# Moving a DFT table set-up, load order and casts in a fused attention and long-convolution kernel

## The chip, the cores and the metric

The kernel runs on one core of a Trainium2 chip. The metric is the device time of one execution in microseconds (us), lower is better. The inputs lie in DRAM as float32; the output goes back as float32.

## The reference

Windowed attention with a few global keys, then a gated long convolution (a circular one, through an FFT over the 768 positions), for 4 batches:

```python
scores = scale * q @ k.T ; keep = is_global | is_local      # 8 global keys, 96 local ones
a = softmax(where(keep, scores + bias_by_head_and_distance, -1e9))
x = a @ v                       # (4, 768, 8 * 64)
proj = x @ w_proj               # 512 -> 3 * 512 : x1, x2, x3
X2 = rfft(x2, axis=1); H = rfft(filter_fft, axis=0)
y = x1 * irfft(X2 * H) * x3
return y @ w_out
```

## The kernel before, in words

**Attention.** A batch has 8 heads of 768 positions, taken as 4 pairs of heads. Keys are cut into 7 tiles of 128 rows: 8 global keys and 120 local ones each (EW, K0 give their widths and starts). The 8 rows of the global keys and values are the same in all tiles; only tile 0 gets them from DRAM, and one DMA on SP's queue copies them to tiles 1 to 6 (L110, `kt<-kt` and `vt<-vt`). A pair goes through transposes of q and k (L434, L459; in batch 0 L449), scores in three groups (L471) with one exp each on ACT (L478), a multiplication by a mask on DVE (L487, L490), two calls of `values` (L498, L503: the product with v and the row sums; then a reciprocal and a multiplication on DVE, L507, L508), and a transpose to `xT` (L515, copied by ACT at L516). After two pairs, DVE forms the sums and differences of the two halves of the sequence, `xa` and `xb` (L424, L425).

**Convolution ("hyena").** Six projections of `xa`, `xb` (L532) give x2; the DFT is a product with a table `fwd` (`forward`, L316, six slots, copied by ACT to `X` at L571); `product` and `sums` on DVE multiply by the filter's spectrum `h1`, `h2` (L558 to L568); the inverse is a product with the table `inv` (L602). Eight `gate` calls give x1 * x3: 8 matmuls each (L545), a scaling on ACT (L549) and a multiplication on DVE (L550). Then `w_out` (L620), a scaling on ACT (L623) and the stores on SP (L624). All six-way users of PSUM share three banks, the tag "mm".

**Tables.** `dft_angles`, `dft_fold` and `dft_sines` make `fwd`: outer products on TensorE (L235 to L241), a rounding copy on ACT (L245), two folding steps on DVE (L250, L253), a sine on ACT (L261, from another activation table than exp). `filter_stage` makes the spectrum (`filter_spectrum`: six `forward` calls on the filter's halves `f2`, each read by ACT and then by DVE) and the inverse tables (`inverse_tables`: transposes of `fwd`).

**Order.** It is written out by hand: each engine runs its instructions in the order in which the program emits them. `weave` merges streams: each has a number of chunks and a stretch from a to b on a common scale, and the chunk that is due first comes next. `after(n, fn)` puts DVE work off by n chunks. `emit` runs the tables first, then batch 0's attention (with `busy`, matmuls on zeros, in between), then for each b the convolution of batch b woven with the attention of batch b+1 (called stage b below). `load_batch(b+1)` is called right before stage b. Loads that change float32 to float16 are issued by GpSimd (POOL); batch 0's q and k come through SP's queue as float32 (`load_first`), six staging tiles for eight loads, and are cast by DVE and ACT (`cast_first`, L140).

A queue or an engine's instruction stream that waits holds all that is behind it. Line numbers are those of the kernel before, unless "now" stands with them.

## Time and profile before

| | |
|---|---|
| time, median of 2 runs | 254.11 us (253.55 to 254.67) |
| profiled execution | 254.49 us, of which its span 252.7 us |
| busy: TensorE (PE), VectorE (DVE) | 201.4 us (80%), 157.5 us (62%) |
| busy: ScalarE (ACT), GpSimd (POOL) | 143.2 us (57%), 78.4 us (31%) |
| DMA | 21.73 MB, mean 86 GB/s |
| mean granted TensorE clock | 0.946 of full speed |
| one load issued by GpSimd (L105) | 0.94 to 0.97 us |
| GpSimd's issues of batch 0's values, of a third of w_proj and of the filter | 6.0 to 15.3 us |

All times in the rows are us from the span's start. The page's shares are means over unlike parts: 11 us of set-up, 39 us of batch 0's attention, stages 0 to 2, and a last convolution that has no attention beside it. PE's busy time includes matmuls that run at half clock and the filling `busy` matmuls. A row of a timeline gives start, duration, engine, line, operation and operands, and in brackets how long the engine had stood idle and what ended it.

### The profile page before, as it was taken

What the parts mean: (1) busy time and instruction counts of PE and PEld (TensorE: products, weight loads), DVE (VectorE), ACT (ScalarE), POOL (GpSimd) and SP (SyncE); (2) the same over time, 40 slices, a digit from 0 to 9 for tenths busy, and PEclk for the clock granted to TensorE, in tenths of its full rate; (3) what the DMA queues carried; (4) which work ended last, traced back from release to release, by engine and by line L of the source; (5) the groups of instructions that cost most, each with busy time, mean ns of one, the idle gap of its engine ahead of it and who ended that gap; (6) DMA issues with size and microseconds to landing.
All of it is one profiled execution on the core that took longest, in us unless ns stands there. A gap on an engine that the chain in (4) does not pass through costs nothing.

```text
span 252.7 us, 4276 instructions
## 1 busy us (share of the span) xinstructions
PE 201.4 (80%) x1670; PEld 107.7 (43%) x1670; DVE 157.5 (62%) x333; ACT 143.2 (57%) x233; POOL 78.4 (31%) x100
## 2 busy tenths in 40 slices
PE   7871777778689779660998989959988989996884
PEld 2330544433345445330355645424644554453431
DVE  6774468725688988520269979714799793067340
ACT  5874247458355667440476577437665666663433
POOL 6960799996780000395820000000000000000000
PEclk9979579999999999995699999999999999999799
DMA  6999999999998000299990000250000004200006
GB/s 212 256 194 205 161 60 135 138 148 164 130 126 38 0 0 3 83 196 190 123 91 3 0 3 0 83 185 0 3 0 3 1 0 178 75 0 0 3 11 238
DMA packets 79628, 21.73 MB, mean 86 GB/s; under 512 B 71336, under 2 KB 76536, under 8 KB 79608
## 3 DMA queue, kind: packets, MB, share of 16 engines
q0 software_dynamic: 73584, 11.67, 70.9%
q1 hardware_dynamic: 6024, 9.79, 11.6%
q8 instruction: 13, 0.21, 0.4%
q14 instruction: 7, 0.06, 0.1%
HBM read 26.48 MB, written 6.29 MB: 130 GB/s over the span
## 4 chain that ended last, share of the span: by engine, by line
PE 31%; DVE 26%; POOL 15%; DMA 15%; ACT 6%; issue 5%; SPq 0%; POOLq 0%; DVEq 0%; ACTq 0%
PE pt L620 7%; PE pt L532 6%; DVE g L550 5%; PE pt L545 5%; POOL vt L105 5%; DMA fl<-in_moe_filter_fft_dram 5%; DMA kt<-kt 4%; DMA qt<-in_q_dram 3%; PE pt L316 3%; POOL kt L105 3%; DVE xn L508 3%; PE tx L515 2%; DMA kt<-in_k_dram 2%; POOL qt L117 2%; PE pt L602 2%
## 5 line engine op out<-in xcount | busy, mean ns | idle before, releaser
L545 PE MATMUL pt<-xT,w 128*128 128x384 f16 x256 | 47.9, 332 | 0.5 <-ACT dst L534 0.4
L545 PEld LDWEIGHTS <-w 128*128 128x128 f16 x256 | 23.8, 99 | 17.6 <-issue 4.2
L478 ACT ACTIVATE E_99<-sp 128x864 f16<-128x864 f32 x24 | 21.5, 898 | 12.4 <-PE sp L471 11.9
L478 ACT ACTIVATE E_96<-sp 128x864 f16<-128x864 f32 x24 | 21.4, 894 | 8.6 <-PE sp L471 6.2
L105 POOL DMA_DIRECT2D vt<-in_v_dram x28 | 26.0, 965 | 0.9 <-issue 0.6
L534 ACT CAST dst<-pt 128x512 f16<-128x512 f32 x24 | 14.0, 585 | 21.0 <-PE pt L532 20.8
L620 PE MATMUL pt<-wo,y 128*128 128x512 f16 x96 | 23.2, 380 | 2.8 <-DVE y L613 2.2
L571 ACT CAST X<-pt 128x512 f16<-128x512 f32 x24 | 14.1, 586 | 16.1 <-PE pt L316 15.9
L602 PE MATMUL pt<-inv,X 128*128 128x384 f16 x96 | 19.5, 334 | 3.8 <-DVE X L568 3.0
L623 ACT ACTIVATE t<-pt 128x512 f32<-128x512 f32 x24 | 14.3, 597 | 14.3 <-PE pt L620 14.1
L269 PE MATMUL pt<-idle 128*128 128x512 f16 x44 | 20.0, 511 | 1.2 <-DVE idle L645 1.2
L471 PE MATMUL sp<-QT,KT 64*128 64x216 f16 (+2 forms) x224 | 18.2, 254 | 3.5 <-ACT E_96 L478 1.8
L508 DVE TENSOR_TENSOR xn<-o,rc 128x448 f16<-128x448 f32 x32 | 20.0, 624 | 1.1
L105 POOL DMA_DIRECT2D kt<-in_k_dram x21 | 19.2, 938 | 4.6 <-DMA qt<-in_q_dram 3.4
L316 PE MATMUL pt<-dst,fwd 128*128 128x512 f16 x72 | 19.0, 380 | 0.0
L515 PE MATMUL tx<-ident,xn 128*128 128x128 f16 x112 | 8.9, 219 | 11.6 <-DVE QT L439 5.7
L516 ACT COPY xT<-tx 128x768 f16<-128x768 f16 x16 | 12.8, 799 | 9.4 <-PE tx L515 9.1
L460 DVE COPY KT<-tk 128x896 f16<-128x896 f16 x12 | 7.4, 619 | 14.4 <-PE tk L459 14.4
L459 PE MATMUL tk<-ident,kt 128*128 128x128 f16 x84 | 7.3, 225 | 11.3 <-DMA kt<-kt 11.3
L117 POOL DMA_DIRECT2D qt<-in_q_dram x18 | 16.0, 962 | 0.0
L471 PEld LDWEIGHTS <-KT 64*128 64x128 f16 x224 | 7.5, 95 | 19.2 <-issue 15.4
L604 ACT CAST eo<-pt 128x384 f16<-128x384 f32 x16 | 7.7, 484 | 12.7 <-PE pt L602 6.8
(228 smaller groups left out, 392.2 us busy)
## 6 DMA issues: line engine op xcount, KB each, us to landing
out_dram<-t SPq DMA_DIRECT2D x24, 256.0 KB, 2.1
vt<-in_v_dram POOLq DMA_DIRECT2D x24, 128.0 KB, 6.4
qt<-in_q_dram POOLq DMA_DIRECT2D x18, 128.0 KB, 6.7
kt<-in_k_dram POOLq DMA_DIRECT2D x18, 128.0 KB, 5.5
t<-in_q_dram SPq DMA_DIRECT2D x4, 384.0 KB, 6.7
t<-in_k_dram SPq DMA_DIRECT2D x4, 384.0 KB, 6.6
w<-in_moe_w_proj_dram POOLq DMA_DIRECT2D x3, 512.0 KB, 13.8
fl<-in_moe_filter_fft_dram POOLq DMA_DIRECT2D x1, 768.0 KB, 12.3
```

What stands on the lines that cost most here:

```text
L105: g.dma_start(dst[P - (hi - lo):P, t, :, 0:D], src[b, :, lo:hi, :].rearrange("h p d -> p h d"))
L117: g.dma_start(qt[:, t], self.q[b, :, P * t:P * t + P, :].rearrange("h p d -> p h d"))
L269: self.nc.tensor.matmul(pt, self.idle[:, 0:P], self.idle, start=True, stop=True)
L316: self.nc.tensor.matmul(pt, self.fwd[:, kt, s, :], src[:, kt, :], start=(kt == 0), stop=(kt == 2))
L471: nc.tensor.matmul(sp[:, hh, off:off + w], KT[64 * hh:64 * hh + 64, o:o + P], QT[64 * hh:64 * hh + 64, KL * m:KL * m + w], start=(off == 0 ...
L478: nc.scalar.activation(eo, sp[:, :, 0:432].rearrange("p h (m w) -> p h m w", m=2), Act.Exp, scale=self.scale)
L508: nc.vector.tensor_mul(xn[:, :, hh, :], o[:, :, 0:D], rc.to_broadcast([P, 7, D]))
L532: nc.tensor.matmul(pt, src[:, c, P * t:P * t + P], self.w[:, c, DM:2 * DM], start=(c == 0), stop=(c == 3))
L545: nc.tensor.matmul(pt[:, 0:h], self.w[:, c, o + P * j:o + P * j + P], xT[:, c, h * s:h * s + h], start=(c == 0), stop=(c == 3))
L602: nc.tensor.matmul(pt[:, 0:h], X[:, s, cs], self.inv[:, s, :], start=(s == slots[0]), stop=(s == slots[-1]))
L620: nc.tensor.matmul(pt, y[:, c, P * t:P * t + P], self.wo[:, c, :], start=(c == 0), stop=(c == 3))
L623: nc.scalar.mul(ot, pt, osc)
```

## The change

It does these things:

- `fwd` is made in `filter_stage`, within stage 0, its pieces woven between the first projections; the table of ACT loaded at the start is that of exp. `filter_stage` has 16 chunks from 0.0 to 0.4 (9 from 0.05 to 0.3 before), and the next attention starts at 0.4 of stage 0 (0.25 before). The filter's halves are formed by DVE, not POOL.
- In stage 0 all eight gates come right after the projections (`early`). Elsewhere the gate after the first pair of `forward` calls comes later, and `halves` is emitted ahead of its gate.
- The loads of batch b+2 are issued before stage b; those of batch 1, and two thirds of `w_proj`, right after batch 0's attention is emitted.
- Batch 0's value rows of the global keys are copied by DVE (one copy of 8 partitions by 3120 elements) in place of the DMA.
- The q and k casts of batch 0's pairs 2 and 3 are made by POOL.
- `values` calls come one or two chunks later than before; the attention in stages 1 and 2 is spread to 0.95 (0.9 before).
- Six `busy` matmuls at the start (2 and 10 before); `distances` first; `later` is kept sorted.

```diff
--- before.py
+++ after.py
@@ -107,8 +107,9 @@
             if t == 0:
                 g.dma_start(dst[0:NG, 0, :, 0:D],
                             src[b, :, 0:NG, :].rearrange("h p d -> p h d"))
-        self.nc.sync.dma_start(dst[0:NG, 1:7], dst[0:NG, 0:1].to_broadcast(
-            [NG, 6] + list(dst.shape[2:])))
+        if b > 0:
+            self.nc.sync.dma_start(dst[0:NG, 1:7], dst[0:NG, 0:1].to_broadcast(
+                [NG, 6] + list(dst.shape[2:])))
 
     def load_batch(self, b):
         g = self.nc.gpsimd
@@ -135,7 +136,9 @@
     def cast_first(self, hp):
         sq, sk = self.first[2 * hp:2 * hp + 2]
         out = []
-        for cp, src in ((self.nc.vector.tensor_copy, sq), (self.nc.scalar.copy, sk)):
+        pool = self.nc.gpsimd.tensor_copy
+        for cp, src in ((pool if hp > 1 else self.nc.vector.tensor_copy, sq),
+                        (pool if hp > 1 else self.nc.scalar.copy, sk)):
...
@@ -154,12 +157,14 @@
     def load_weights(self):
         g, cp, DM = self.nc.gpsimd, self.cp, self.DM
         self.w = cp.tile([P, 4, 3 * DM], F16)
-        wr = self.w_proj.rearrange("(t p) n -> p t n", p=P)
-        g.dma_start(self.w[:, :, DM:2 * DM], wr[:, :, DM:2 * DM])
+        self.wr = self.w_proj.rearrange("(t p) n -> p t n", p=P)
+        g.dma_start(self.w[:, :, DM:2 * DM], self.wr[:, :, DM:2 * DM])
         self.fl = self.mp.tile([P, 6, DM], F16, tag="g", bufs=2)
         g.dma_start(self.fl, self.filt.rearrange("(t p) n -> p t n", p=P))
-        g.dma_start(self.w[:, :, 0:DM], wr[:, :, 0:DM])
-        g.dma_start(self.w[:, :, 2 * DM:3 * DM], wr[:, :, 2 * DM:3 * DM])
+
+    def load_more_weights(self):
+        for o in (0, 2 * self.DM):
+            self.nc.gpsimd.dma_start(self.w[:, :, o:o + self.DM], self.wr[:, :, o:o + self.DM])
 
     def load_w_out(self):
         self.wo = self.cp.tile([P, 4, self.DM], F16)
@@ -240,8 +245,9 @@
                                  skip_group_check=True)
             nc.tensor.matmul(o, one, cst[:, None, 0:2, None].to_broadcast([1, 2, 2, r]),
                              start=False, stop=True, skip_group_check=True)
-        tag = ("y", "eo", "ab", "ab")[a]
-        th = self.mp.tile(list(an.shape), F32, tag=tag, bufs=2 if tag == "ab" else 1, name="th")
+        if a == 0:
+            self.th = self.mp.tile([P, 3, 512], F32, tag="y", bufs=1)
+        th = self.th[:, a] if a < 3 else self.mp.tile([P, 768], F32, tag="eo", bufs=1, name="th")
@@ -292,6 +298,7 @@
     def after(self, n, fn):
 
         self.later.append((self.chunk + n, fn))
+        self.later = deque(sorted(self.later, key=lambda x: x[0]))
...
-    def filter_halves(self):
-        f2 = self.mp.tile([P, 2, 3, self.DM], F16, tag="y", bufs=1)
-        self.nc.gpsimd.tensor_add(f2[:, 0], self.fl[:, 0:3], self.fl[:, 3:6])
-        self.nc.gpsimd.tensor_sub(f2[:, 1], self.fl[:, 0:3], self.fl[:, 3:6])
-        self.f2 = f2
-
     def filter_stage(self):
+        self.fwd = self.cp.tile([P, 3, 6, P], F16)
+        ths = []
+        for a in range(4):
+            ths.append(self.dft_angles(a))
+            for k in range(2):
+                self.after(k + 1, lambda k=k, a=a: self.dft_fold(k, *ths[a]))
+            yield 1
+        yield 1
+        yield 1
+        for a in range(4):
+            self.dft_sines(a, ths[a][0])
         yield from self.filter_spectrum()
         yield from self.inverse_tables()
 
@@ -332,6 +344,10 @@
 
 
         nc, cp, DM = self.nc, self.cp, self.DM
+        f2 = [self.mp.tile([P, 3, DM], F16, tag="stg", bufs=6, name="f2") for _ in range(2)]
+        nc.vector.tensor_add(f2[0], self.fl[:, 0:3], self.fl[:, 3:6])
+        nc.vector.tensor_sub(f2[1], self.fl[:, 0:3], self.fl[:, 3:6])
+        yield 1
         self.h1 = cp.tile([P, 6, DM], F16)
         self.h2 = cp.tile([P, 6, DM], F16)
         sc = 2.0 * H_SCALE
@@ -354,7 +370,7 @@
                 nc.vector.tensor_scalar(self.h2[0:64, s], pt[64:P], sc, None, op0=Alu.mult)
...
         for s in range(6):
-            self.forward(s, self.f2[:, 0], self.f2[:, 1], evac)
+            self.forward(s, f2[0], f2[1], evac)
             yield 1
 
 
@@ -404,13 +420,16 @@
         trk(0)
         yield 1
         for i in range(n + 1):
+            if first and i == 1:
+                self.nc.vector.tensor_copy(vt[0:NG, 1:7], vt[0:NG, 0:1].to_broadcast(
+                    [NG, 6, self.H, self.D + 1]))
             for live, fn in ((i < n, lambda: sc(i, 0)),
                              (i + 2 < n and first, lambda: cast(i + 2)),
-                             (i > 0, lambda: val(i - 1, 0)),
                              (i + 1 < n, lambda: trk(i + 1)),
                              (i < n, lambda: sc(i, 1)),
+                             (i > 0, lambda: val(i - 1, 0)),
+                             (i + 1 < n, lambda: trq(i + 1)),
                              (i > 0, lambda: val(i - 1, 1)),
-                             (i + 1 < n, lambda: trq(i + 1)),
                              (i < n, lambda: sc(i, 2)),
                              (i > 0, lambda: trx(i - 1))):
                 if live:
@@ -520,9 +539,24 @@
...
-    def hyena(self, b, xT, xa, xb):
+    def hyena(self, b, xT, xa, xb, early=False):
         nc, mp, DM, S = self.nc, self.mp, self.DM, self.S
         h = S // 2
+        g = mp.tile([P, 4, S], F16, tag="g", bufs=2)
+
+        def gate(j, s):
+            p1 = self.mm()
+            p3 = self.mm()
+            for pt, o in ((p1, 0), (p3, 2 * DM)):
+                for c in range(4):
+                    nc.tensor.matmul(pt[:, 0:h], self.w[:, c, o + P * j:o + P * j + P],
+                                     xT[:, c, h * s:h * s + h],
+                                     start=(c == 0), stop=(c == 3))
+            x1 = mp.tile([P, h], F16, tag="x1", name="x1")
+            nc.scalar.mul(x1, p1[:, 0:h], X1_SCALE)
+            nc.vector.tensor_mul(g[:, j, h * s:h * s + h], p3[:, 0:h], x1)
+
+        gates = iter([(j, s) for j in range(4) for s in range(2)])
         ab = []
         for src in (xa, xb):
             dst = mp.tile([P, 3, DM], F16, tag="ab", bufs=2)
@@ -534,20 +568,10 @@
                 nc.scalar.copy(dst[:, t, :], pt)
                 yield 1
             ab.append(dst)
-
-        g = mp.tile([P, 4, S], F16, tag="g", bufs=2)
-
-        def gate(j, s):
...
+        if early:
+            for js in gates:
+                gate(*js)
+                yield 1
 
         X = mp.tile([P, 6, DM], F16, tag="X", bufs=1)
 
@@ -572,17 +596,22 @@
             if s % 2 == 1:
                 self.after(1, lambda: product(s))
 
-        gates = iter([(j, s) for j in range(4) for s in range(2)])
-        gate(*next(gates))
-        yield 1
+        def more():
+            js = next(gates, None)
+            if js:
+                gate(*js)
+            return js
+
+        if more():
+            yield 1
         for s in range(6):
             self.forward(s, ab[0], ab[1], evac)
             yield 1
-            if s % 2 == 1:
-                gate(*next(gates))
+            if s % 2 == 1 and s > 1 and more():
                 yield 1
-        gate(*next(gates))
-        yield 1
+        for _ in range(2):
+            if more():
+                yield 1
 
         y = mp.tile([P, 4, S], F16, tag="y", bufs=1)
 
@@ -604,12 +633,12 @@
                 nc.scalar.copy(eo[:, jj, 0], pe[:, 0:h])
                 nc.scalar.copy(eo[:, jj, 1], po[:, 0:h])
                 yield 1
-            gate(*next(gates))
             halves(jp, eo)
+            more()
             js = slice(2 * jp, 2 * jp + 2 - jp)
             nc.vector.tensor_mul(y[:, js, :], y[:, js, :], g[:, js, :])
             yield 1
-        gate(*next(gates))
+        more()
         nc.vector.tensor_mul(y[:, 3, :], y[:, 3, :], g[:, 3, :])
         yield 1
 
@@ -652,41 +681,34 @@
             self.E.append(et)
         warm = self.sp.tile([1, 2], F32, bufs=1)
         nc.vector.memset(warm, 0.0)
-        nc.scalar.activation(warm, warm, Act.Sin)
-        self.busy(2)
-        self.fwd = cp.tile([P, 3, 6, P], F16)
-        self.dft_rows()
+        nc.scalar.activation(warm, warm, Act.Exp)
+        self.busy(6)
+        self.distances()
         self.ident = cp.tile([P, P], F16)
         make_identity(nc, self.ident)
-        self.distances()
-        ths = [self.dft_angles(a) for a in range(4)]
-        self.busy(10)
-        for k in range(5):
-            for j, a in ((0, k), (1, k - 1)):
-                if 0 <= a < 4:
-                    self.dft_fold(j, *ths[a])
+        self.dft_rows()
         cast = self.cast_first(0)
-        for a in range(4):
-            self.dft_sines(a, ths[a][0])
         self.masks(0)
         self.masks(1)
         qkv = self.batch_tiles()
         self.load_tiles(qkv[2], self.v, 0)
         self.load_weights()
-        self.filter_halves()
         x = self.new_x()
         self.weave((self.attention(*qkv, *x, first=cast), 33, 0, 1))
+        self.load_more_weights()
+        loads = [qkv, self.load_batch(1)]
+        self.load_w_out()
         for b in range(self.B):
-            streams = [(self.hyena(b, *x), 30, 0, 1)]
+            streams = [(self.hyena(b, *x, early=(b == 0)), 30, 0, 1)]
             nx = None
             if b == 0:
-                streams.insert(0, (self.filter_stage(), 9, 0.05, 0.3))
+                streams.insert(0, (self.filter_stage(), 16, 0.0, 0.4))
+            if b + 2 < self.B:
+                loads.append(self.load_batch(b + 2))
             if b + 1 < self.B:
-                qkv = self.load_batch(b + 1)
-                if b == 0:
-                    self.load_w_out()
                 nx = self.new_x()
-                streams.insert(0, (self.attention(*qkv, *nx), 33, 0.25 if b == 0 else 0.0, 0.9))
+                streams.insert(0, (self.attention(*loads[b + 1], *nx), 33,
+                                   0.4 if b == 0 else 0.0, 0.95))
             self.weave(*streams)
```

On SP's queue, before, the piece from batch 1's copies on; kt_1421 and vt_1422 are batch 2's tiles, out_0_dram the stores of batch 0:

```order
L110 DMA vt_677<-vt_677 8x6x520
L624 DMA out_0_dram<-t_1321 128x512
L624 DMA out_0_dram<-t_1357 128x512
L624 DMA out_0_dram<-t_1393 128x512
L624 DMA out_0_dram<-t_1401 128x512
L624 DMA out_0_dram<-t_1409 128x512
L624 DMA out_0_dram<-t_1417 128x512
L110 DMA kt_1421<-kt_1421 8x6x512
L110 DMA vt_1422<-vt_1422 8x6x520
```

The same piece now, where kt_623 and vt_624 are batch 1's tiles, kt_653 and vt_654 batch 2's:

```order
L111 DMA kt_623<-kt_623 8x6x512
L111 DMA vt_624<-vt_624 8x6x520
L111 DMA kt_653<-kt_653 8x6x512
L111 DMA vt_654<-vt_654 8x6x520
L653 DMA out_0_dram<-t_1386 128x512
```

Batch 2's two copies stood behind the six stores of batch 0; now they stand ahead of them.

On ACT, at the start of stage 0, before (dst: the projections; h_721, h_722: the spectrum):

```order
L534 CAST dst<-pt 128x512 x2
L341 ACTIVATE h_721<-pt 128x512
L344 ACTIVATE h_721<-pt 1x512
L534 CAST dst<-pt 128x512
L346 ACTIVATE h_722<-pt 128x512
```

And now (th: the angles; fwd: the sines; h_767: the spectrum):

```order
L251 ACTIVATE th<-pt 128x512
L568 CAST dst<-pt 128x512
L251 ACTIVATE th<-an 128x768
L568 CAST dst<-pt 128x512 x2
L267 ACT_TABLE_LOAD
L267 ACTIVATE fwd<-th 128x512 x3
L267 ACTIVATE fwd<-th 128x3x256
L568 CAST dst<-pt 128x512
L357 ACTIVATE h_767<-pt 128x512
```

The spectrum's first copy stood behind two projections; now it stands behind all six, the table load and the four sines.

On DVE, in batch 0's attention, now, where the first `values` needs E_96 and vt (before, no vt copy stood here, and the K transposes of pair 2, rows L472 to L474 now, came after the first reciprocal):

```order
L506 TENSOR_TENSOR E_96<-E_96,mask 128x2x216 x2
L424 COPY vt<-vt 8x3120
L509 TENSOR_TENSOR E_96<-E_96,mask 128x2x2x216
L509 TENSOR_TENSOR E_99<-E_99,mask 128x2x2x216
L472 COPY KT<-tk 128x6x120
L473 COPY KT<-tk 128x120
L474 COPY KT<-KT 128x7x8
L526 RECIPROCAL rc<-o 128x7
```

The copy stands ahead of the last mask of pair 0 and of all that follows on DVE.

## Rows read from the trace of the kernel before

**Rows 1.** Stretches (us): busy of PE, PEld, DVE, ACT, POOL; granted clock; DMA.

```profile
11.12:50.20 39.08, 25.94 (x269) 14.94 (x268) 25.08 (x53) 21.05 (x27) 29.12 (x31) 0.83 1.59 152
50.20:70.07 19.87, 15.18 (x88) 7.07 (x87) 10.20 (x17) 11.28 (x20) 16.64 (x21) 1.00 2.34 146
70.07:111.40 41.33, 34.64 (x356) 20.24 (x354) 32.55 (x70) 25.78 (x42) 10.89 (x14) 1.00 0.64 53
119.60:167.00 47.40, 44.30 (x394) 24.03 (x394) 33.57 (x71) 29.41 (x50) 7.44 (x9) 0.96 0.79 58
170.00:214.00 44.00, 41.04 (x384) 22.75 (x385) 33.02 (x70) 28.56 (x48) 0.00 (x0) 1.00 0.06 21
214.00:252.70 38.70, 30.91 (x154) 15.23 (x152) 14.71 (x27) 18.75 (x35) 0.00 (x0) 0.96 0.16 60
178.00:208.00 30.00, 27.21 (x280) 15.91 (x278) 26.73 (x57) 18.89 (x34) 0.00 (x0) 1.00 0.01 1
```

**Rows 2.** The chain of waits, its two stalls between stages: start, duration.

```profile
111.43 8.05 DMA kt<-kt
...
166.93 2.90 DMA kt<-kt
```

**Rows 3.** Timeline of SP's queue.

```profile
20.70 0.88 SPq L110 DMA_DIRECT2D vt<-vt  x1
...
103.78 7.36 SPq L624 DMA_DIRECT2D out_dram<-t  x6
111.43 1.36 SPq L110 DMA_DIRECT2D kt<-kt  x1
```

**Rows 4.** Timeline of PE: first and last angle matmul, two waits in batch 0.

```profile
2.77 0.60 PE L235 MATMUL pt<-row 1*128 1x512 f16 x1 [0.55 <-DVE row L216]
...
6.54 0.41 PE L241 MATMUL an<-cst,one 1*128 1x256 f16 x1
...
26.64 0.24 PE L498 MATMUL o<-vt,E_96 128*128 128x65 f16 x1 [5.81 <-DMA vt<-vt]
...
34.35 0.55 PE L515 MATMUL tx<-ident,xn 128*128 128x128 f16 x7 [1.72 <-DVE QT L436]
```

**Rows 5.** Timeline of ACT and DVE at the end of the set-up.

```profile
7.69 0.82 ACT L140 CAST t<-t 128x768 f16<-128x768 f32 x1
...
8.41 2.40 ACT L261 ACTIVATE fwd<-th 128x512 f16<-128x512 f32 x4
...
9.79 0.55 DVE L140 CAST t<-t 128x768 f16<-128x768 f32 x1
...
10.82 1.28 ACT L202 ACT_TABLE_LOAD   x1
```

**Rows 6.** Timeline of DVE and POOL: a copy within SBUF, POOL's first filter half.

```profile
2.98 0.39 DVE L186 COPY dm<-dg 128x432 f32<-128x432 f32 x1 [0.26 <-POOL dg L181]
...
26.77 3.09 POOL L322 TENSOR_TENSOR f_231<-fl 128x1536 f16<-128x1536 f16 x1 [9.96 <-DMA fl<-in_moe_filter_fft_dram]
```

**Rows 7.** Line L487 from 26 to 50 us: durations in ns, min/median/max.

```profile
L487 DVE TENSOR_TENSOR E_99<-E_99,mask x4: 371/374/1617, 31.5 to 46.6; 128x432 f16<-128x432 f16 x4
```

**Rows 8.** Timeline of DVE in stage 0: first and last evacuation of the spectrum.

```profile
54.43 0.69 DVE L342 TENSOR_SCALAR h_721<-pt 128x512 f16<-128x512 f32 x1 [2.37 <-ACT h_721 L341]
...
64.25 0.69 DVE L355 TENSOR_SCALAR h_722<-pt 64x512 f16<-64x512 f32 x1
```

**Rows 9.** The chain of waits in the last convolution.

```profile
214.00 5.18 PE pt L532 x24
...
234.46 2.38 PE pt L545 x8
...
239.72 1.31 PE pt L545 x8
...
241.12 0.56 DVE g L550
```

**Rows 10.** Timeline of PE: the wait there before the inverse DFT.

```profile
232.05 2.41 PE L602 MATMUL pt<-inv,X 128*128 128x384 f16 x10 [2.16 <-DVE X L568]
```

More of the change, by code (lines that the diff above doesn't have):

```diff
@@ L521, in mm @@
         return pt
-    def hyena(self, b, xT, xa, xb):
+    def hyena(self, b, xT, xa, xb, early=False):
         nc, mp, DM, S = self.nc, self.mp, self.DM, self.S
         h = S // 2
-        ab = []
-        for src in (xa, xb):
-            dst = mp.tile([P, 3, DM], F16, tag="ab", bufs=2)
-            for t in range(3):
-                pt = self.mm()
-                for c in range(4):
-                    nc.tensor.matmul(pt, src[:, c, P * t:P * t + P], self.w[:, c, DM:2 * DM],
-                                     start=(c == 0), stop=(c == 3))
-                nc.scalar.copy(dst[:, t, :], pt)
-                yield 1
-            ab.append(dst)
         g = mp.tile([P, 4, S], F16, tag="g", bufs=2)
@@ L550, in gate @@
             nc.vector.tensor_mul(g[:, j, h * s:h * s + h], p3[:, 0:h], x1)
+        gates = iter([(j, s) for j in range(4) for s in range(2)])
+        ab = []
+        for src in (xa, xb):
+            dst = mp.tile([P, 3, DM], F16, tag="ab", bufs=2)
+            for t in range(3):
+                pt = self.mm()
+                for c in range(4):
+                    nc.tensor.matmul(pt, src[:, c, P * t:P * t + P], self.w[:, c, DM:2 * DM],
+                                     start=(c == 0), stop=(c == 3))
+                nc.scalar.copy(dst[:, t, :], pt)
+                yield 1
+            ab.append(dst)
+        if early:
+            for js in gates:
+                gate(*js)
+                yield 1
         X = mp.tile([P, 6, DM], F16, tag="X", bufs=1)
@@ L580, in hyena @@
             yield 1
-            if s % 2 == 1:
-                gate(*next(gates))
+            if s % 2 == 1 and s > 1 and more():
                 yield 1
-        gate(*next(gates))
-        yield 1
+        for _ in range(2):
+            if more():
+                yield 1
         y = mp.tile([P, 4, S], F16, tag="y", bufs=1)
```

## The prediction

> **What bounds the kernel now.** I read the busy time by stretches first, then the chain of waits, then the timelines at the places that it names. The stretches [rows 1] show one kernel with unlike parts. Stage 2 (170 to 214 us) is the full pipeline: 44.0 us, of which TensorE is busy for 41.04, with VectorE at 26.73 of 30.0 us in its middle. Both are close to full there, and little is to be won. Batch 0's attention takes 39.08 us with TensorE busy for 25.94 at a mean clock of 0.83. Stage 0 takes 61.2 us (50.20 to 111.40), and its second part, from the first scores at 70.07 on, is VectorE's: 32.55 us of 41.33 (79%). Stage 1 takes 47.40 us where stage 2 takes 44.00.
>
> Between the stages the chain [rows 2] has two plain stalls, 8.05 and 2.90 us, both on the copy of the global keys. SP's queue [rows 3] says why: the first of these copies is issued at 111.43, when the six stores of batch 0 are out (103.78 to 111.14). Its data had been in place long before. For stage 1 the price is more than the wait: the clock of 119.60 to 167.00 is 0.96, against 1.00 in stage 2 [rows 1].
>
> In batch 0 [rows 3, 4] all values have landed by 20.70, when SP issues the copy of the global value rows; the product that needs it starts at 26.64, after 5.81 us of idle TensorE. The chain also runs through GpSimd's issuing of batch 1's loads up to 67 us. I do not count that as a bound, as batch 0's own instructions fill TensorE's time there.
>
> **The change part by part**, against the profiled execution: 254.49 us, of which 252.7 us span and 1.8 us around it. The median of the two runs, 254.11, is 0.4 below it.
>
> 1. *The stalls between stages.* With batch 2's copies ahead of batch 0's stores on SP, and batch 3's ahead of batch 1's, nothing late stands before them. What they wait for now is their loads. Batch 2's need batch 0's value buffer, free at about 44 us, and 22 issues of GpSimd at about 0.95 us, 21 us: in place by 75, needed after 110. Batch 3's need batch 1's buffers, free near 108, and are needed near 155. So 8.05 + 2.90 go, and with the first stall the slow start of stage 1, 47.40 - 44.00 = 3.40. Together **-14.35**. Bounds: the slow start could come from elsewhere (-10.95) and nothing more than all of it can go.
>
> 2. *Batch 0's attention.* The set-up loses the folds and sines: VectorE casts q at 9.79, behind the folds, while ScalarE's cast of k shows that the data were there by 7.69, and the table load and sines of 2.40 and 1.28 us leave ScalarE as well [rows 5]. That start, 2.5 us earlier, does not reach the end, since the values still land at about 20.7. Then VectorE copies 3120 elements on 8 partitions. No row has this copy. The nearest is 0.39 us for 432 float32 elements [rows 6]: at that rate 2.8, at no cost but the start 0.2; I take 2.0, nearer the row. It stands ahead of pair 0's last mask, two halves of 0.374 in another row [rows 7]: 0.7. The first product then starts at 20.7 + 2.0 + 0.7 = 23.4, not 26.64: -3.2. From there to the first transpose of x it took 34.35 - 26.64 = 7.7 us [rows 4]. One score group and pair 2's K transposes now stand before that product and not behind it, about 1.3 us, and GpSimd's filter halves are gone, during which one mask took 1.617 us instead of 0.374 [rows 7]: 1.2 more. So 5.2, and the rest as before. **-5.7**; bounds -9 (the copy nearly free, higher clock) and -1 (below).
>
>    The four casts on GpSimd start when its issues of the values and two weights are done, at 15.3. Its nearest row is 3.09 us for 1536 elements with two inputs [rows 6], half of that for 768: 1.55 each, 15.3 to 21.5, with pair 2's two done at 18.4, a little before they hold the scores up. Hidden behind the values. At 3.09 each they would end at 27.7. One mask was held by a GpSimd instruction for 1.2 us [rows 7], and the masks of pairs 0 and 1 fall beside the casts now. The Trainium skill (SBUF — State Buffer, Who interferes with whom) has the rule: a VectorE instruction with two SBUF inputs and a GpSimd one that reads SBUF exclude each other for a whole instruction; the row agrees, and by the rule the casts bring back what the filter halves took.
>
> 3. *Stage 0* takes up what leaves the set-up. Its first part, up to the first scores, is 19.87 us now [rows 1]. After the change:
>    - projections and angles: 24 projection matmuls take 5.18 [rows 9], the angles 6.95 - 2.77 = 4.2 [rows 4]; with the start 9.7 us. The folds and rounding copies run beside them.
>    - the spectrum's first matmul needs the sines, and these stand on ScalarE behind five of six projections: about 9.5 + 1.28 + three of four sines, 1.9 = 12.7. TensorE waits 3.0 us. For ScalarE's table switch the row is 1.28, and the exp after it starts at once. The Trainium skill (ScalarE: Activation LUTs, What ACT_TABLE_LOAD costs) adds a drain of some 1.4 us to each switch; by it stage 0's two switches would take 2.8 us longer. The row shows no such time.
>    - the spectrum: VectorE's evacuation waits for ScalarE's each time, and six of them took 53.8 to 64.94 = 11.1 us [rows 8]. Three gates stand between the six now, with a fourth around them: their 0.5 us on ScalarE and 0.56 on VectorE [rows 9] lengthen that to about 13, until 26.4.
>    - four more gates at 1.31 [rows 9], the inverse tables and the first transposes of batch 1: 7.5. The first scores come at 33.9.
>
>    That is +14.0. The second part loses seven gates: VectorE's 32.55 less 7 x 0.56 is 28.6. At this stretch's own share (79%) that is 36.2 us, at stage 2's (89%) 32.1; I take 35.4, as the moved `values` should close a little of its idle time: -5.9. Stage 0: **+8.1**, 69.3 us. Bounds: +2 if only the angle matmuls (4.2) stay and the closer packing takes 2 of them back; +14 if the second part gains nothing.
>
> 4. *Stages 1 and 2*: the same instructions, TensorE at 93%. Later `values` and gates can win or lose part of 3 us of idle time each: **-0.6**, bounds -3 and +2.
>
> 5. *The last convolution* (38.70 us): three gates after the last `forward` in place of two, so that the wait of 2.16 us before the inverse [rows 10] is filled by 1.31 us of work that had stood in front. The clock then need not fall: eight gate matmuls took 2.38 us there and 1.31 a little later [rows 9], and ten of the inverse some 0.8 too much. 1.3 + 1.07 + 0.8: **-3.0**, bounds -4 and 0.
>
> 6. Batch 1's loads about 9 us earlier, `busy` matmuls, sorting: 0. What hides the loads is the first part of stage 0; they are in place by 50 us where the transposes want them at 75. If they came 25 us later it would cost all that is beyond that.
>
> Sum: -14.35 - 5.7 + 8.1 - 0.6 - 3.0 = -15.5, so 254.49 - 15.5 = **239.0 us**.
>
> **The rivals.**
> - *Stage 0 takes the tables nearly free*: +1 in place of +8.1, **232**. For it: TensorE idles 4.7 us in the first part and 6.7 in the second [rows 1]. Against it: the moved gates leave a part where VectorE binds for one where the evacuations do.
> - *The port between VectorE and GpSimd decides batch 0*: casts of 3.09 us hold up the last mask by one cast, +3: **242**. For it: the mask of 1.617 us [rows 7]. Against it: the masks have some 5 us until the values are there. The rule is that of the Trainium skill's page SBUF — State Buffer, as above.
> - *Stage 0 costs more*: the wait for the sines lowers the clock, as the wait before the inverse did [rows 9, 10], while the gates are on the path, and the sparser second part stays at 41 us: +6 and +4, **249**.
> - *The stalls stay*: if batch 2's or 3's loads are late, the copies wait ahead of the stores and hold these too. Term 1 goes: **253**. Against it: 30 us of room.
> - *Slower*: TensorE runs stage 0 at 1.2 GHz for most of its length. Its work there is 15.18 + 34.64 + 4.2 = 54 us at the full clock; it decides once half-clock work outgrows the 15 us of slack in 69.3, and with all of it at half (the gates' 2.38 for 1.31) the stage takes about 98, **268**. To end over 259 four fifths must run so. For it: batch 0, sparse as well, had 0.83 [rows 1]. Against it: the second part with TensorE at 84% kept 1.00, and no slow stretch lasted that long.
>
> **How the numbers follow.** A measurement of this kernel can tell about 2% from no change, 5 us: below 249.0 is faster, above 259.2 slower. The forecast has 0.60 (233 to 246 by its bounds, which do not all fall on one side), the nearly free stage 0 has 0.12, the port 0.08, the costly stage 0 0.12, the stalls 0.04, slower 0.04. The range takes the forecast, most of the cheap case and the port: 231 to 247. Faster: 0.60 + 0.12 + 0.08 + half of 0.12 = 0.86; same 0.10; slower 0.04.
>
> **What would show it.** Right: no TensorE wait on kt between stages and clock 1.00 in stage 1; first product of batch 0 at 23 to 24 us; first scores of batch 1 some 34 us after the first projection, with a wait of about 3 us for the sines; stage 0 near 69 us; no slow matmuls before the inverse of the last batch. Wrong: a VectorE copy over 3 us, GpSimd casts over 3 us each, a stage 0 below 64 or above 74 us, or SP's copies issued after a store of the batch before.

## The result, and the profile after

The changed kernel takes **242.09 us** (median of 2 runs, 241.84 to 242.33) where the kernel before takes 254.11: a ratio of 0.953, 95% interval 0.943 to 0.963. The forecast was 239.0. The profiled execution has a span of 240.6 us, 12.1 less than before. A few executions, mostly of the kernel before, ran some per cent longer at a lower granted clock, and the times and ratios of the experiments leave them out.

I cut the span where each stage's first projection starts (in stage 0: the first angle matmul). These are the stretches of the changed kernel, with the same columns as [rows 1]: batch 0's attention, stage 0 up to batch 1's first scores, stage 0's second part, stages 1 and 2, the last convolution.

```profile
6.34:44.49 38.15, 27.91 (x269) 15.89 (x269) 26.73 (x52) 18.10 (x24) 31.11 (x38) 0.87 2.20 191
44.49:77.57 33.08, 27.26 (x156) 13.24 (x157) 20.99 (x33) 19.93 (x35) 20.92 (x26) 0.95 2.23 119
77.57:118.81 41.24, 30.50 (x300) 17.58 (x300) 29.00 (x62) 24.48 (x37) 7.30 (x10) 0.83 0.24 24
118.81:162.60 43.79, 41.71 (x397) 23.43 (x395) 33.09 (x71) 30.07 (x51) 11.85 (x14) 1.00 1.26 99
162.60:206.22 43.62, 41.37 (x391) 23.09 (x389) 33.08 (x71) 29.94 (x50) 0.00 (x0) 1.00 0.10 35
206.22:240.60 34.38, 29.06 (x155) 14.81 (x153) 14.69 (x27) 18.94 (x35) 0.00 (x0) 1.00 0.19 69
```

| cut at the first projections (us) | before | after | moved | forecast |
|---|---|---|---|---|
| up to stage 0 | 50.22 | 44.49 | -5.7 | -5.7 |
| stage 0, first part | 19.85 | 33.08 | +13.2 | +14.0 |
| stage 0, second part | 40.25 | 41.24 | +1.0 | -5.9 |
| stages 1 and 2 with their stalls | 103.51 | 87.41 | -16.1 | -14.95 |
| last convolution | 38.87 | 34.38 | -4.5 | -3.0 |

One row is wrong: the second part of stage 0, by 7 us. The other four rows came out 3.4 us better than forecast in sum, the last convolution by 1.5, and this hid half of that miss.

SP's queue (timeline: start, duration, instruction) answers to [rows 3]. Batch 2's two copies, at 65.92 and 74.32, now go out before the stores of batch 0, and the two TensorE waits on the copies of `kt` between the stages, 8.05 and 2.90 us, are gone.

```profile
43.75 0.88 SPq L111 DMA_DIRECT2D kt<-kt  x1
51.48 0.69 SPq L111 DMA_DIRECT2D vt<-vt  x1
65.92 0.69 SPq L111 DMA_DIRECT2D kt<-kt  x1
74.32 0.69 SPq L111 DMA_DIRECT2D vt<-vt  x1
113.86 5.95 SPq L653 DMA_DIRECT2D out_dram<-t  x6
132.73 0.71 SPq L111 DMA_DIRECT2D kt<-kt  x1
```

In batch 0 the first product with the values runs on from 21.25 (timeline of PE; in brackets the idle time and what ended it), where [rows 4] had 26.64. TensorE's first transpose comes at 6.34 instead of 11.12, since the tables are no longer made ahead of it. The first row is that of the kernel before, the others are of the changed one.

```profile
11.12 0.55 PE L434 MATMUL tq<-ident,t 128*128 128x128 f16 x6
...
6.34 0.82 PE L453 MATMUL tq<-ident,t 128*128 128x128 f16 x6 [2.41 <-DVE t L143]
...
21.25 0.19 PE L517 MATMUL o<-vt,E_96 128*128 128x65 f16 x1 [1.87 <-DVE vt L424]
...
26.50 0.95 PE L534 MATMUL tx<-ident,xn 128*128 128x128 f16 x7
```

In stage 0 the spectrum's first matmul waits for the sines. It starts 10.6 us into the stage (55.05 less 44.49); before (first row), it started at 52.95, 2.7 us in.

```profile
52.95 0.81 PE L316 MATMUL pt<-f_231,fwd 128*128 128x512 f16 x3
...
55.05 2.46 PE L323 MATMUL pt<-f_757,fwd 128*128 128x512 f16 x6 [1.76 <-ACT fwd L267]
```

And before the last inverse, where [rows 10] had 2.16 us of idle time and half clock:

```profile
223.16 1.80 PE L631 MATMUL pt<-inv,X 128*128 128x384 f16 x10 [0.88 <-DVE X L592]
```

### The profile page after: what moved, and what is told of

It reads as the page before. It is cut to its first block, busy times and chain, and to the rows that moved or that the text cites. A ratio compares the mean times of both kernels' runs of the same rounds, so it can differ in the third digit from the quotient of the medians.

```text
span 240.6 us, 4274 instructions
## 1 busy us (share of the span) xinstructions
PE 200.6 (83%) x1664; PEld 108.8 (45%) x1664; DVE 161.1 (67%) x334; ACT 144.4 (60%) x232; POOL 75.2 (31%) x102
## 4 chain that ended last, share of the span: by engine, by line
PE 47%; DVE 23%; ACT 10%; issue 3%; ACTq 0%; DVEq 0%
PE pt L552 9%; PE pt L566 9%; PE pt L649 8%; PE pt L631 5%; PE pt L323 4%; DVE g L557 3%; DVE xn L527 3%; PE sp L490 3%; ACT E_99 L497 3%; PE tx L534 2%; PE o L517 2%; PE o L522 1%; PE tk L478 1%; PE tq L453 1%; DVE X L592 1%
## 5 line engine op out<-in xcount | busy, mean ns | idle before, releaser
L649 PE MATMUL pt<-wo,y 128*128 128x512 f16 x96 | 24.4, 396 | 2.6 <-DVE y L642 2.6
L105 POOL DMA_DIRECT2D vt<-in_v_dram x28 | 25.1, 911 | 2.6 <-DMA kt<-in_k_dram 1.2
L631 PE MATMUL pt<-inv,X 128*128 128x384 f16 x96 | 20.6, 351 | 3.7 <-DVE X L592 3.6
L275 PE MATMUL pt<-idle 128*128 128x512 f16 x38 | 17.7, 503 | 1.2 <-DVE idle L674 1.2
L534 PE MATMUL tx<-ident,xn 128*128 128x128 f16 x112 | 9.8, 232 | 8.1 <-DVE xn L527 8.1
L118 POOL DMA_DIRECT2D qt<-in_q_dram x18 | 15.9, 904 | 0.2 <-issue 0.2
L96 POOL MEMSET vt<- 128x56 f16 x4 | 1.6, 412 | 43.3 <-PE o L522 43.3
L649 PEld LDWEIGHTS <-y 128*128 128x128 f16 x96 | 9.1, 102 | 13.2 <-DVE y L642 4.0
L631 PEld LDWEIGHTS <-X 128*128 128x128 f16 x96 | 8.9, 103 | 11.1 <-DVE X L592 4.7
```

The lines of the kernel that those rows point to most:

```text
L105: g.dma_start(dst[P - (hi - lo):P, t, :, 0:D], src[b, :, lo:hi, :].rearrange("h p d -> p h d"))
L118: g.dma_start(qt[:, t], self.q[b, :, P * t:P * t + P, :].rearrange("h p d -> p h d"))
L275: self.nc.tensor.matmul(pt, self.idle[:, 0:P], self.idle, start=True, stop=True)
L534: nc.tensor.transpose(tx[:, KL * t:KL * t + P], xn[:, t, :, :], self.ident)
L631: nc.tensor.matmul(pt[:, 0:h], X[:, s, cs], self.inv[:, s, :], start=(s == slots[0]), stop=(s == slots[-1]))
L649: nc.tensor.matmul(pt, y[:, c, P * t:P * t + P], self.wo[:, c, :], start=(c == 0), stop=(c == 3))
```

## The experiments

Each was timed in three rounds on one of two chips; the ratio is to the kernel before on the same chip (means 253.9 to 254.5 us there). Instructions that are the same in several kernels do not take the same time in each profile: batch 0's attention, the same up to there, ends at 50.2 to 52.0 us in the kernel before and the two made from it, and at 44.0 to 45.7 in the changed kernel and the four that differ from it in stage 0 alone. Stage 0's second part repeats better: 41.24, 41.05 and 40.68 us in the three profiles that have the changed kernel's stage 0. Differences of one or two us between single profiles are read with this in mind.

**The load order alone, on the kernel before** (b_loads_ahead).

```diff
-            if b + 1 < self.B:
-                qkv = self.load_batch(b + 1)
-                if b == 0:
-                    self.load_w_out()
+            if b == 0:
+                loads = [qkv, self.load_batch(1)]
+                self.load_w_out()
+            if b + 2 < self.B:
+                loads.append(self.load_batch(b + 2))
+            if b + 1 < self.B:
```

> The kernel before with the load order alone changed: batch 2's loads and copies are issued ahead of stage 0, batch 3's ahead of stage 1. Theory of term 1 (the copies stood behind the stores on SP's queue): both stalls between stages go and stage 1 runs at clock 1.00, so 14.35 us less, about 239.8 us. Rival (the copies wait for something else, or GpSimd's and the queue's waits move elsewhere): at most one stall goes, 245 to 254 us.

240.0 us, ratio 0.948 (0.940 to 0.956): 13.3 less in the mean, as the queue theory said to within about 1 us. Batch 2's copies are issued at 75.37 and 82.51 (SP's timeline), 23 us ahead of the first store:

```profile
75.37 0.69 SPq L110 DMA_DIRECT2D kt<-kt  x1
82.51 0.69 SPq L110 DMA_DIRECT2D vt<-vt  x1
105.57 7.45 SPq L624 DMA_DIRECT2D out_dram<-t  x6
```

The loads themselves are not what moved: GpSimd issues the last six of batch 2's values from 69.47 on in the kernel before (first row) and from 69.87 on here.

```profile
69.47 5.32 POOL L105 DMA_DIRECT2D vt<-in_v_dram  x6
...
69.87 2.69 POOL L105 DMA_DIRECT2D vt<-in_v_dram  x3
```

Stages 1 and 2, cut at their first projections, in the kernel before (first two rows) and here (last two; columns of [rows 1]):

```profile
110.32:165.80 55.48, 44.30 (x397) 24.04 (x395) 33.57 (x71) 29.86 (x51) 14.05 (x17) 0.91 0.98 79
165.80:213.83 48.03, 42.00 (x391) 23.12 (x389) 33.58 (x71) 29.61 (x50) 0.00 (x0) 1.00 0.10 34
...
112.11:157.28 45.17, 42.18 (x398) 23.46 (x396) 33.50 (x71) 29.73 (x51) 14.04 (x17) 1.00 1.20 95
157.28:202.09 44.81, 41.84 (x392) 23.12 (x390) 33.59 (x71) 29.59 (x50) 0.00 (x0) 1.00 0.10 36
```

They lose 10.31 and 3.22 us, 13.5 in all. So this one edit is worth as much as the whole change (240.0 against 242.09, intervals that overlap). All the others together bring nothing that can be told; some must cost what others win.

**The order of the gates alone, on the kernel before** (b_gate_order).

```diff
-            if s % 2 == 1:
+            if s % 2 == 1 and s > 1:
                 gate(*next(gates))
                 yield 1
-        gate(*next(gates))
-        yield 1
+        for _ in range(2):
+            gate(*next(gates))
+            yield 1
...
-            gate(*next(gates))
             halves(jp, eo)
+            gate(*next(gates))
```

> The kernel before with the order of the gates alone changed (none after the first pair of forward calls, two after the last; halves ahead of the gate). Theory of term 5: the wait before the last inverse goes, its clock stays at 1.00, the last convolution takes 34 to 36 us in place of 38.7, stages 1 and 2 unchanged: 3 to 4.5 us less, 250 to 251 us. Rival (the shorter last convolution comes from stage 2's tail or the sorted order): 254 us.

249.09 us, ratio 0.981 (0.974 to 0.988). The last convolution (same columns as [rows 1]) takes 34.25 us, as in the changed kernel, at clock 1.00, 4.6 less than before. That is all of it: the whole kernel is 4.6 us faster in the mean, a little more than the theory's range.

```profile
213.95:248.20 34.25, 29.05 (x155) 14.78 (x153) 14.69 (x27) 18.94 (x35) 0.00 (x0) 1.00 0.19 69
```

**Late gates in stage 0** (a_gates_late).

```diff
-            streams = [(self.hyena(b, *x, early=(b == 0)), 30, 0, 1)]
+            streams = [(self.hyena(b, *x), 30, 0, 1)]
```

> The changed kernel with stage 0's eight gates where the other stages have them, not ahead of the spectrum. Theory A (the second part of stage 0 is as long with or without them, since VectorE's order and TensorE's falling clock fill what they leave): the first part gets about 7 x 1.3 us shorter, the second stays near 41 us or grows by up to 4: 5 to 8 us less, 234 to 237 us. Theory B (the gates' VectorE time of 3.9 us and TensorE time of 9 us come back in full in the second part): 242 us, no change.

234.93 us, ratio 0.926 (0.920 to 0.932). The size is theory A's, the place is not. The first part is no shorter (34.15), since the six `forward` calls of batch 0 took the gates' places in it; the second part fell from 41.24 to 32.80, at clock 1.00.

```profile
45.74:79.89 34.15, 25.22 (x126) 10.87 (x126) 22.02 (x36) 19.89 (x34) 20.61 (x25) 0.90 2.37 116
79.89:112.69 32.80, 29.10 (x330) 17.83 (x331) 27.20 (x59) 24.75 (x38) 3.73 (x6) 1.00 0.15 36
```

**Filling matmuls in stage 0's attention** (a_filled).

```diff
+                    self.busy(fill)
                     yield 1
...
+        if early:
+            self.busy(10)
         for jp in range(2):
             eo = mp.tile([P, 2, 2, h], F16, tag="eo", bufs=1)
...
-                streams.insert(0, (self.attention(*loads[b + 1], *nx), 33,
+                streams.insert(0, (self.attention(*loads[b + 1], *nx, fill=int(b == 0)), 33,
```

> The changed kernel with filling matmuls on zeros in stage 0's attention, one of 0.22 us after each of 33 pieces and ten before the first inverse, so that TensorE has less idle time there. Theory C (the second part of stage 0 lost its gain to TensorE's lower clock, 0.83): clock near 1.00 there and 3 to 5 us less, about 238 us. Theory D (VectorE's order binds there whatever the clock): clock up, time the same or up to 4 us more, 242 to 246 us.

240.27 us, ratio 0.947 (0.941 to 0.954, which overlaps the changed kernel's interval). The clock of the second part rose from 0.83 to 1.00 and the part fell from 41.24 to 39.58: 1.7 us, a quarter of the 7 us that are missing and less than theory C had. The 40 filling matmuls take their own places in TensorE's order, so the 1.7 us are what the clock gives back less what they cost; the clock's full price may be higher.

```profile
78.80:118.38 39.58, 34.77 (x340) 18.88 (x340) 29.16 (x62) 24.66 (x37) 6.32 (x8) 1.00 0.19 19
```

**Late gates with the attention from 0.25** (a_late_att25): the edit of a_gates_late, and this one.

```diff
-                                   0.4 if b == 0 else 0.0, 0.95))
+                                   0.25 if b == 0 else 0.0, 0.95))
```

> The changed kernel with late gates (as in a_gates_late) and the attention of stage 0 starting at 0.25 of the weave, as before, in place of 0.4. Theory E (what counts in stage 0 is that batch 0's forward calls are made in the first part, before batch 1's attention): a start at 0.25 puts them behind attention again, stage 0 gets longer, 236 to 239 us. Theory F (the gates' place alone counts): 235 us, or less by the better overlap.

238.3 us, ratio 0.938 (0.931 to 0.946), in theory E's range. First part 21.75, second 48.80: 3.6 us more in sum than with 0.4.

**Late gates, tables in the set-up** (a_late_tables_first): `filter_stage` without its angles, folds and sines, these again ahead of batch 0's attention with the first table that of sine and the kernel before's 12 filling matmuls in place of six; the late gates; and the streams' numbers:

```diff
-                streams.insert(0, (self.filter_stage(), 16, 0.0, 0.4))
+                streams.insert(0, (self.filter_stage(), 10, 0.05, 0.3))
...
-                                   0.4 if b == 0 else 0.0, 0.95))
+                                   0.25 if b == 0 else 0.0, 0.95))
```

> Late gates, and the tables back in the set-up as in the kernel before (angles, folds, sines, with its 12 filling matmuls, stage 0's streams at its numbers: filter 0.05 to 0.3, attention from 0.25, to 0.95). Theory of terms 2 and 3 (the set-up has room for the tables, since batch 0 waits for its values anyway, and stage 0 has none): batch 0's attention ends at 45 to 47 us, stage 0 takes about 60 us in place of 67, so 228 to 231 us. Rival (the set-up's 2.5 us come back in full in batch 0's attention, stage 0 gains only the angles' 4 us): 233 to 235 us.

**227.68 us**, ratio 0.895 (0.888 to 0.902), the fastest, below both kernels. Stage 0 takes 20.86 + 38.39 = 59.25; the next-nearest kernel, a_late_att25, differs by the tables and the filter's numbers and takes 70.55. Batch 0's attention ends at 45.17, 1.2 later than there, which is within the scatter given above.

```profile
45.17:66.03 20.86, 14.99 (x88) 7.14 (x88) 12.04 (x19) 11.53 (x20) 17.51 (x22) 1.00 2.65 145
66.03:104.42 38.39, 33.87 (x352) 19.84 (x350) 31.74 (x69) 25.14 (x41) 6.86 (x9) 1.00 0.62 48
```

**The tables alone back in the set-up** (a_tables_first): as above, with the early gates, the filter's 10 chunks from 0.05 to 0.4, attention from 0.4.

> The changed kernel with its early gates, and the tables alone back in the set-up (with its 12 filling matmuls; the filter's stream from 0.05 to 0.4, batch 1's attention from 0.4 as in the changed kernel). From the pair a_late_att25 and a_late_tables_first: stage 0's first part loses the angles and the wait for the sines, 6 to 9 us; batch 0's attention ends within 1.5 us of the changed kernel's. So 233 to 236 us. Rival (the block of gates fills that room, since the spectrum's evacuation binds): 239 to 242 us.

231.4 us, ratio 0.912 (0.903 to 0.920), below the range of the theory. Stage 0 takes 26.73 + 38.24 = 64.97, 9.35 less than in the changed kernel. Its set-up fills time in which batch 0 waits for its values: the attention ends at 42.94, no later than the changed kernel's 44.49.

**The copy of batch 0's value rows by DMA** (a_vt_dma).

```diff
-        if b > 0:
-            self.nc.sync.dma_start(dst[0:NG, 1:7], dst[0:NG, 0:1].to_broadcast(
-                [NG, 6] + list(dst.shape[2:])))
+        self.nc.sync.dma_start(dst[0:NG, 1:7], dst[0:NG, 0:1].to_broadcast(
+            [NG, 6] + list(dst.shape[2:])))
...
-            if first and i == 1:
+            if False:
```

> The changed kernel with batch 0's copy of the global value rows made by the DMA on SP's queue again, not by VectorE. Theory of term 2: the first product with the values waits for the DMA, starts near 26 us in place of 22, and batch 0's attention ends 3 to 5 us later: 245 to 247 us. Rival (the values' landing or VectorE's order binds, not the copy): 242 us.

245.36 us, ratio 0.966 (0.959 to 0.973): 3.3 more than the changed kernel. The product waits until 26.96 again (timeline of PE):

```profile
26.96 0.24 PE L516 MATMUL o<-vt,E 128*128 128x65 f16 x1 [5.28 <-DMA vt<-vt]
```

**All casts on VectorE and ScalarE** (a_casts_back).

```diff
-        for cp, src in ((pool if hp > 1 else self.nc.vector.tensor_copy, sq),
-                        (pool if hp > 1 else self.nc.scalar.copy, sk)):
+        for cp, src in ((self.nc.vector.tensor_copy, sq),
+                        (self.nc.scalar.copy, sk)):
```

> The changed kernel with all casts of q and k on VectorE and ScalarE, none on GpSimd. In the changed kernel two half masks took 3.52 us beside GpSimd's casts, 0.75 us elsewhere. Theory G (they wait for the port, but the values' landing at 20.2 covers it): the masks take 0.75, the time stays within 1 us, 241 to 243 us. Theory H (the held masks are on the path): 238 to 240 us. Rival (VectorE and ScalarE need the room): 243 to 245 us.

242.24 us, ratio 0.955 (0.946 to 0.965): no change. The pair of masks takes 0.67 us in it, then VectorE waits 5.17 us for the values (timeline of DVE; the first two rows are the changed kernel's, the last two this one's). In the changed kernel the pair takes 3.52 us beside GpSimd's casts and VectorE still waits 1.27 us. Theory G holds as far as the time goes: the masks are held, and the values' landing covers it.

```profile
15.46 3.52 DVE L506 TENSOR_TENSOR E_96<-E_96,mask 128x432 f16<-128x432 f16 x2
20.24 0.96 DVE L424 COPY vt<-vt 8x3120 f16<-8x3120 f16 x1 [1.27 <-DMA vt<-in_v_dram]
...
15.10 0.67 DVE L506 TENSOR_TENSOR E<-E,mask 128x432 f16<-128x432 f16 x2
20.95 1.08 DVE L424 COPY vt<-vt 8x3120 f16<-8x3120 f16 x1 [5.17 <-DMA vt<-in_v_dram]
```

**The forward calls ahead of the block of gates** (a_fwd_first).

```diff
-        if early:
-            for js in gates:
-                gate(*js)
-                yield 1
...
         for s in range(6):
             self.forward(s, ab[0], ab[1], evac)
             yield 1
...
+        if early:
+            for js in gates:
+                gate(*js)
+                yield 1
```

> The changed kernel with stage 0's eight gates still in one block, but the six forward calls of batch 0 ahead of the block, not behind it. Theory E (the second part of stage 0 is long because batch 0's forward calls, products, inverse and output follow one another there with batch 1's attention between): the forward calls are made in the first part, and the second part loses most of what the late gates won, 3 to 7 us less, 235 to 239 us. Rival (the block of gates itself costs, wherever it stands): 241 to 243 us.

239.61 us, ratio 0.940 (0.932 to 0.948), 0.6 above the range of theory E and 2.5 below the changed kernel, with intervals that overlap. The stretches are clearer: the second part falls from 41.24 to 36.59, the first grows from 33.08 to 34.81. So the place of the `forward` calls counts, but for part of what late gates win.

```profile
44.38:79.19 34.81, 24.74 (x127) 10.43 (x127) 23.75 (x39) 20.96 (x35) 21.25 (x26) 0.92 2.14 115
79.19:115.78 36.59, 31.30 (x331) 19.37 (x331) 25.93 (x56) 23.61 (x37) 7.05 (x10) 0.93 0.25 26
```

## Why the prediction was right, and where it was not

The measured 242.09 us lies in the stated range, 3.1 us above the forecast. That it lies so near is in part luck: stage 0 took 6.1 us more than its term, and the other terms came out 2.7 us better in sum and hid part of that. One of the prediction's own signs of being wrong, "a stage 0 [...] above 74 us", came true: 33.08 + 41.24 = 74.32.

1. *The stalls between stages.* Right in mechanism, nearly so in size: -14.35 forecast, 13.5 measured for that edit alone in its trace and 13.3 in the times. The slow start went with the first stall: in the kernel before the granted clock is 0.50 from 120 to 122 us, behind the stall, and in b_loads_ahead stage 1 runs at 1.00 throughout. It loses 2.3 us beyond the stall of 8.05 there, where 3.40 was forecast.

2. *Batch 0's attention.* The sum, -5.7, was met, but its terms were mis-sized both ways, so this is luck too. The start came 4.8 us earlier, not 2.5. The copy of 3120 elements took 0.96 us, not 2.0; the wait for the values ended at 20.24, as thought. The first product runs on at 21.25 where 23.4 was forecast, and the first transposes of x follow 5.25 us later, as forecast. What was left "as before" took 18.0 us (26.50 to 44.49) in place of 15.9, and ate that gain. TensorE's clock there was 0.83 against 0.89 before; in a_late_att25, with the same instructions at 0.95, it took 16.5. The casts took 0.84 us each, not 1.55, and were as harmless as forecast. The copy is on the path (a_vt_dma, 3.3 us).

3. *Stage 0.* The first part was right: 33.08 us against 33.9, with 1.76 us of waiting for the sines against 3.0. The step that failed is the second part: "At this stretch's own share (79%) that is 36.2 us, at stage 2's (89%) 32.1; I take 35.4". VectorE's sum there was right (29.00 us, forecast 28.6), its share was not: 70%. I took a share measured with seven gates woven in as a property of VectorE. With the gates gone, all six of batch 0's `forward` calls, the products, the inverse and the output follow one another in this part, one behind the other and behind attention's pieces. Before, two of the six stood in the first part and gates stood between the others; the prediction counted the gates that leave but not the two `forward` calls that stay behind:

```profile
64.37 0.81 PE L316 MATMUL pt<-dst,fwd 128*128 128x512 f16 x3
67.52 0.81 PE L316 MATMUL pt<-dst,fwd 128*128 128x512 f16 x3
```

   The inverse now waits for its products, 2.72 us (last row), where it did not wait before (first row). That wait is there in all four kernels that have early gates ahead of the `forward` calls and no filling (2.5 to 3.4 us), and in neither a_fwd_first nor a_gates_late.

```profile
86.75 1.14 PE L602 MATMUL pt<-inv,X 128*128 128x384 f16 x6
...
94.99 1.46 PE L631 MATMUL pt<-inv,X 128*128 128x384 f16 x4 [2.72 <-DVE X L592]
```

   The clock falls as well. The granted clock is still 1.00 from 88 to 89 us, in which TensorE does nothing, and 0.50 (1.2 GHz) in every microsecond from 91 to 100; filling matmuls bring 1.7 us back.

```profile
88.00:89.00 1.00, 0.00 (x0) 0.00 (x0) 0.97 (x3) 0.43 (x1) 0.00 (x0) 1.00 0.00 0
92.00:93.00 1.00, 0.27 (x1) 0.00 (x0) 1.00 (x3) 0.00 (x0) 0.00 (x0) 0.50 0.00 0
```

   The calls moved ahead give 4.65 us in this part (and cost 1.73 in the first), gates woven back in give 8.4. In the chain of waits of the changed kernel the output's last twenty matmuls stand alone at the end of the stage, where stage 0 ended with sixteen before (third row) and ends with eight in a_gates_late:

```profile
94.25 0.70 DVE X L592
...
113.90 4.74 PE pt L649 x20
...
106.69 3.47 PE pt L620 x16
```

   A term was also left out: the sum has one table load, for the sines, but the exp of batch 1's first scores needs the other table, and this second load stands in the chain at the head of the second part. TensorE's next scores wait for that exp. a_tables_first, which has no table load in stage 0, has a second part 3.0 us shorter, at clock 0.96.

```profile
77.53 1.28 ACT L497 ACT_TABLE_LOAD   x1
...
79.77 0.36 PE L490 MATMUL sp<-QT,KT 64*128 64x216 f16 x4 [0.69 <-ACT E_96 L497]
```

   How the 8.4 us of late gates divide between the earlier `forward` calls, the clock and the output beside attention is not settled: the first gave 4.65 in a run that also moved the gates, and the 1.7 of the clock is net of the filling.

   The rival "stage 0 costs more" had half of this: the sparser second part staying at 41 us. It priced that at +4, where its own figures make 5.6 (41 less 35.4). Its other half did not come: the wait for the sines left the first part at clock 0.95 and shorter than forecast.

4. *Stages 1 and 2.* Mis-sized: 43.79 and 43.62 us, where b_loads_ahead, which has the load order alone, takes 45.17 and 44.81. So the rest of the change won 2.6 us there, not 0.6. The order of the gates alone won 0.35 us in these two stages (b_gate_order: 103.16 us against 103.51); that the later `values` won the rest is likely but not shown.

5. *The last convolution.* Right in mechanism, mis-sized: -4.5 against -3.0 (its terms add up to 3.2), and b_gate_order shows that the order of the gates does all of it. The wait before the inverse fell from 2.16 to 0.88. From the start of the inverse on 3.2 us more went: the half-clock matmuls, as counted, and two things that were not, a wait of 0.78 us within the second half of the inverse (this row, of the kernel before) and 0.6 us in the output.

```profile
239.07 0.65 PE L602 MATMUL pt<-inv,X 128*128 128x384 f16 x3 [0.78 <-ACT eo L604]
```

The net of the whole change hides two losses that the runs single out: tables in stage 0 cost 10.7 us (242.09 against 231.4), early gates 7.2 (against 234.93). The two overlap: with both put back the gain is 14.4 us (a_late_tables_first, which also has other stream numbers), not 17.9. What is then left of the change, apart from the load order, is worth as much again as the load order: that kernel is 26.6 us faster than the kernel before, b_loads_ahead 13.3. The tables' loss is not the 4.2 us of angles: of it, 6.35 us lie in the first part and 3.0 in the second. That the first part's share comes from the spectrum, whose evacuation is a chain of its own and starts 10.6 us into the stage instead of 2.7, so that it no longer runs beside the projections, is argued from the trace; no run separates it from the wait for the sines, and a_tables_first also has other filling matmuls and stream numbers.

## What to carry to other kernels

In this kernel a copy issued on SP's queue behind stores waited for the stores' producers, however early its data were there; emitting it ahead of them was worth 13 us, as much as the whole change. Set-up work that looked like a serial prologue cost nothing that the runs could tell while the first stage waited for its data, and moving it into a full stage made it a price; ask first what the prologue is waiting for. The busy share of an engine in one mix of work is not its share in another: when independent work is taken out of a stretch, look for the chain that it was covering.
